# Eight edits to the order of work in a hash-masked attention with a gated feed-forward layer on one core

## The chip, the core and the metric

The kernel runs on one core of a Trainium2 chip. The metric is device time in microseconds (us) of one execution, lower is better. The core has the engines TensorE (PE, with its weight loads shown apart as PEld), VectorE (DVE), ScalarE (ACT), GpSimd (POOL) and SyncE (SP), each with its own queue that is worked off in the order of the program. SP issues most of the transfers (DMAs); POOL issues those of the feed-forward weights.

## The reference

Two stages follow each other. The first is attention in which a query sees only the keys whose six sign bits under a random projection are the same as its own:

```python
q_bits = (einsum('bhsd,dk->bhsk', q, proj) > 0)      # B, H, S, D = 4, 8, 768, 64; six bits
k_bits = (einsum('bhsd,dk->bhsk', k, proj) > 0)
mask = bucket(q_bits)[..., :, None] == bucket(k_bits)[..., None, :]
scores = where(mask, q @ k.T / sqrt(D), -1e9)
attn = softmax(scores);  x = attn @ v                # then heads side by side: 3072 x 512
```

The second is a normalised, gated feed-forward layer on the 3072 rows of x (512 wide, 1536 inside):

```python
xn = x / sqrt(mean(x * x) + 1e-6) * rms_g
out = (silu(xn @ w_gate) * (xn @ w_val)) @ w_out
```

## The kernel before, in words

**Units and slots.** The queries are cut into eight units w of 384 rows (batch w // 2, half w % 2). A unit has eight heads, and a head's 384 queries meet its 768 keys in three slots of two score matmuls (`scores`, L348) and one exponential over 768 columns (`probs`, L358). The 192 slots stand in the list `SLOTS` (L33 to L36); the first units share batches, so their pairs of heads alternate.

**The mask.** It isn't a separate step: twelve rows of sign bits are put below the 64 rows of q and of k in the tile `QK`, so that one matmul over 76 rows gives the score and, for each bit that differs, a large penalty. The bits come from small matmuls into `d_ps` (L214) and a comparison on DVE (`signs`, L221), and they have to be moved to other partitions. For the second, third and fourth pair of heads of batch 1 the function `hash_lone` (L278) moves them with eight transfers on SP (L289), four for each head. The batches before and after have functions of their own.

**Loads.** q and k come as four block transfers a pair of heads each (`load_blocks`, L126), v as one (`load_rows`, L116). DVE turns q and k (`turn_dve`, L198), POOL casts them into `QK` (`cast_pool`, L206). POOL also casts v (`v_prep`, L314) and adds up its rows (`v_sum`, L320 to L322); a matmul with ones makes the mean of v out of these sums (`v_mean`, L329), and DVE scales it into `cvb` (L332). The two halves of w_out are issued by POOL (`load_wo`, L543) in slots 36 and 52.

**Out of the attention.** `av` (L370) multiplies the probabilities with v into the one bank pair `o_ps`. `attn_out` adds `cvb` (L385, DVE), takes a reciprocal (L390, DVE), scales into x (L394) and squares (L406). The last two run on POOL, for the pair "urgent" (unit 0, heads 6 and 7) on DVE, where the squares are added up in the same instruction (L401). `sumsq` (L410, DVE) adds up the squares that POOL made, some slots later.

**The norm and the feed-forward part.** `norm` (L417 on DVE, L419 and L423 on POOL) makes the factors `rstd`; `scale_x` makes `xn` on DVE (L434, or L429 with the gain multiplied in); `turn_x` turns it: four transposes a chunk of 128 rows on PE (L448) with a copy on DVE (L449), or, in the units of `BY_DMA`, for two of three chunks, eight transfers with transposition on SP (L441). Then `gate` (L463 and a tanh on ACT, L465), `value` (L473, with two steps on DVE, L474 and L475) and `project` (L486, a copy on ACT, L493, and a store on SP, L495). All these matmul results share three PSUM banks in rotation (`gps`), so a new one waits until the third one before it has been read.

**The order** is written out by hand. `at(s, f, ...)` puts a step into slot s with a rank; L731 to L741 go through the slots, issue the scores of the next slot, the steps of rank below 3, the exponential, and the other steps in the order of rank and entry. Nothing reorders it afterwards: an instruction that waits holds up all that stands behind it on its engine, and a transfer on SP that waits for its source holds up the transfers behind it. The table `work` (L659) has, for each pair of heads of batches 1 to 3, the slots of its three loads, of its turns and of its hash.

**The tail.** The last 128 rows of the output are made by L743 to L759 in two halves of 256 columns.

Of the kernel before, what the change touches and what calls it, by code (L numbers as in the profile page):

```python
# [40 lines left out]
BY_PE = [(0, hp) for hp in range(4)] + [(1, 0)]  # L41


BY_DMA = (3, 4, 5)


@with_exitstack
def kernel(
# [12 lines left out]
    nc = tc.nc  # L61
# [30 lines left out]
    wo = const.tile([128, NF, DMODEL], FP16, name="wo")  # L92
# [118 lines left out]
    def hash_bank(parts):  # L211
        ps = bank("d_ps", [128, HALF])
        for t, (w, src) in enumerate(parts):
            nc.tensor.matmul(  # L214
                ps[32 * t : 32 * t + 32, :], w, src,
                start=True, stop=True, tile_position=(0, 32 * t),
            )
        return ps

    def signs(bt, ps):  # L220
        nc.vector.tensor_scalar(  # L221
            out=bt, in0=ps, scalar1=thr, scalar2=scl, op0=ALU.is_gt, op1=ALU.mult
        )
# [6 lines left out]
    def bits_tile(i):  # L230

        if i % 2 == 0:
            held.append(spool.tile([128, S], FP16, name="bits", bufs=3))
        return held[-1][:, (i % 2) * HALF : (i % 2 + 1) * HALF]
# [43 lines left out]
    def hash_lone(b, hp):  # L278

        ps = hash_bank(  # L280
            [(w[:, 0:32], T0[b, hp, which][:, half * HALF : (half + 1) * HALF])
             for half in range(2) for w, which in ((pk, "k"), (pq, "q"))]
        )
        bt = bits_tile(0)
        signs(bt, ps)
        for hh in range(2):
            for half, j in ((0, 0), (0, 1), (1, 1), (1, 0)):
                p0, o = 64 * half + 32 * j + 12 * hh, (S, 0)[j] + half * HALF
                nc.sync.dma_start(  # L289
                    out=QK[b, hp][D:KROWS, hh, o : o + HALF], in_=bt[p0 : p0 + 12]  # L290
                )

    def hash_pairs(b, hps):

        bt = spool.tile([128, S], FP16, name="bits", bufs=3)
        for half in range(2):
            cs = slice(half * HALF, (half + 1) * HALF)
            ps = hash_bank(
                [(w, T0[b, hp, which][:, cs])
                 for hp in hps for w, which in ((pk[:, 0:32], "k"), (pq[:, 0:32], "q"))]  # L300
            )
            signs(bt[:, cs], ps)
        for i, hp in enumerate(hps):
            for hh in range(2):
                for j, o in enumerate((S, 0)):
                    p0 = 64 * i + 32 * j + 12 * hh
                    nc.sync.dma_start(
                        out=QK[b, hp][D:KROWS, hh, o : o + S], in_=bt[p0 : p0 + 12]
                    )
# [26 lines left out]
    x, ssp, xn, xnT, ht = {}, {}, {}, {}, {}  # L336
# [41 lines left out]
    def attn_out(w, hp):  # L378
        b = w // 2
        if w not in x:  # L380
            x[w] = xpool.tile([128, 3, DMODEL], FP32, name="x")
            ssp[w] = xpool.tile([128, 3, 4], FP32, name="ssp")
        o = ot.pop((w, hp))
        tmp = spool.tile([128, 3, 2, 66], FP32, name="otmp")
        nc.vector.tensor_add(  # L385
            tmp[:, :, :, 0:65], o[:, :, :, 0:65],
            cvb[b % 2][:, 2 * hp : 2 * hp + 2, 0:65].unsqueeze(1).to_broadcast([128, 3, 2, 65]),
        )
        r = spool.tile([128, 3, 2, 1], FP32, name="rcp")
        nc.vector.reciprocal(r, tmp[:, :, :, 64:65])  # L390
        xd = x[w][:, :, 128 * hp : 128 * hp + 128]
        urgent = (w, hp) == (0, 3)
        eng = nc.vector if urgent else nc.gpsimd
        eng.tensor_mul(  # L394
            xd.rearrange("p c (h d) -> p c h d", h=2), tmp[:, :, :, 0:64],
            r.to_broadcast([128, 3, 2, 64]),
        )
        sq = spool.tile([128, 3, 128], FP32, name="sq")
        if urgent:
            for c in range(3):  # L400
                nc.vector.scalar_tensor_tensor(  # L401
                    out=sq[:, c], in0=xd[:, c], scalar=1.0, in1=xd[:, c],
                    op0=ALU.mult, op1=ALU.mult, accum_out=ssp[w][:, c, hp : hp + 1],
                )
        else:
            nc.gpsimd.tensor_mul(sq, xd, xd)  # L406
        return sq
# [17 lines left out]
    def scale_x(w, c):  # L425
        if w not in xn:
            xn[w] = npool.tile([128, 3, DMODEL], FP16, name="xn")
        if w in BY_DMA and c < 2:
            nc.vector.scalar_tensor_tensor(  # L429
# [6 lines left out]
    def turn_x(w, c):  # L436
        if w not in xnT:
            xnT[w] = npool.tile([128, 4, HALF], FP16, name="xnT", bufs=2)
        if w in BY_DMA and c < 2:
            for kt in range(4):  # L440
# [154 lines left out]
    def at(s, f, *a, rank=3):  # L595
        plan[s].append((rank, len(plan[s]), lambda: f(*a)))
# [4 lines left out]
    moves = {}  # L601
# [54 lines left out]
    def in_row(loads, s, hash_slot=None):  # L656
        return loads, range(s, s + 8), (s + 4, s + 8, s + 9), hash_slot

    work = {  # L659
        (1, 1): in_row((21, 22, 32), 42, 51), (1, 2): in_row((34, 35, 37), 49, 58),  # L660
        (1, 3): in_row((38, 40, 44), 56, 65),
        (2, 0): in_row((53, 55, 59), 64), (2, 1): in_row((66, 67, 68), 73, 82),
        (2, 2): in_row((72, 75, 78), 82), (2, 3): in_row((79, 83, 87), 90, 99),
        (3, 0): in_row((88, 91, 98), 100), (3, 1): in_row((94, 97, 112), 110, 119),
# [2 lines left out]
    for (b, hp), (loads, turns, cast_slots, sh) in work.items():  # L667
        for which, s in zip("kqv", loads):
            at(s, load_rows if which == "v" else load_blocks, nc.sync, b, hp, which)
        for i, s in enumerate(turns):  # L670
            at(s, turn_dve, b, hp, "kq"[i // 4], i % 4, rank=5)
        for which, s in zip("kq", cast_slots):
            at(s, cast_pool, b, hp, which)
        if sh:
            if b == 1:
                at(sh, hash_lone, b, hp)
            else:
                at(sh, hash_pairs, b, (hp - 1, hp))
        at(cast_slots[2], v_prep, b, hp)
        at(cast_slots[2], v_sum, b, hp)  # L680
        if b > 1 and hp % 2:
            at(48 * b + (17 if hp == 3 else -4), v_mean, b, hp - 1, 4)
    for hp, s in enumerate((48, 62, 64, 78)):
        at(s, v_mean, 1, hp, 2)

# [15 lines left out]
    for w in range(8):  # L701
        for h in range(H):
            end = LAST[w, h] + (2 if (w, h) == (0, 7) else 3)
            at(end - 1, av, w, h, 0, 9)
            at(end, av, w, h, 9, 18)
            if h % 2:
                at(end, o_step, w, h // 2, rank=4.5)
                if (w, h) != (0, 7):
                    late = 3 if h == 7 and w < 6 else 5 if (w, h) == (0, 5) else 4
                    at(end + late, s_step, w, h // 2, rank=5 if late != 5 else 4)  # L710
        s0 = 24 * w + 42
        n0 = {0: 11, 2: 7, 3: 13, 4: 13, 5: 13}.get(w, 11)
        at(s0 - n0, norm, w, rank=5)
        for c in range(3):
            scale, rank = {0: 6, 2: 6 - c}.get(w, 8 - c), 1
            turn = {0: (4, 3, 2), 2: (4, 2, 1)}.get(w, (5, 3, 1))[c]
            if w in BY_DMA and c < 2:
                scale, turn, rank = 11 - c, 11 - c, 6
            at(s0 - scale, scale_x, w, c, rank=5)
            at(s0 - turn, turn_x, w, c, rank=rank)  # L720
        seen = set()
        for ft in range(NF):
            for f, s in ((g_step, s0 + 16 * ft // NF), (v_step, s0 + (32 * ft + 16) // (2 * NF))):
                at(s, f, w, ft, rank=4 if s in seen else 2)
                seen.add(s)
        for i in range(9 if w < 7 else 6):
            c, j = divmod(i, 3)
            at(s0 + 16 + i, project, w, c, 4 * j, 4 * j + 4, rank=1 if i == 8 else 3)
# [11 lines left out]
        for _, _, f in todo[n:]:  # L740
            f()  # L741
    rows = out[3 * S : 4 * S, :].rearrange("(p c) n -> p c n", c=6)[:, out_chunk(7, 2), :]
    for i in range(2):  # L743
        cs = slice(256 * i, 256 * i + 256)
        y = bank("y_ps")
        for ft in range(NF):
            nc.tensor.matmul(  # L747
                y[:, cs], ht[7][:, ft, 256:384], wo[:, ft, cs],
                start=(ft == 0), stop=(ft == NF - 1),
            )  # L750
        ysb = spool.tile([128, DMODEL], FP32, name="ysb", bufs=3)
        if i == 0:
            nc.scalar.copy(ysb[:, 0:256], y[:, cs])
            nc.sync.dma_start(out=rows[:, cs], in_=ysb[:, 0:256])
        else:
            nc.scalar.copy(ysb[:, 0:128], y[:, 256:384])
            nc.vector.tensor_copy(ysb[:, 128:256], y[:, 384:512])
            nc.scalar.dma_start(out=rows[:, 256:384], in_=ysb[:, 0:128])
            nc.sync.dma_start(out=rows[:, 384:512], in_=ysb[:, 128:256])  # L759


# [28 lines left out]
```

## Time and profile before

| what | value |
|---|---|
| time, three runs | 334.0, 334.08, 335.57 us; median 334.08 |
| span of the profiled execution, first to last instruction | 332.5 us |
| what lies outside that span, against the median | 1.6 us |
| DVE, ACT, POOL busy | 234.2, 208.0, 157.1 us |
| instructions | 7788 |
| moved by DMA | 32.41 MB, mean 97 GB/s |
| PE work, the largest groups | scores 93.7, v_ps 78.1, y_ps 69.2, g_ps 63.4, o_ps 56.7 us |

"Busy" is the time in which an engine had at least one instruction under way; it says nothing about how fast that instruction ran. A row of the timeline gives start, length, engine, line, operation, the tile written and the tile read, shapes, the count of merged instructions, and in brackets the idle time of the engine ahead of it with what ended it. A row of the chain of waits gives start, length and what the end of the program was waiting for then. "SPq" and "POOLq" are instructions of an engine's sequencer; for a transfer, the length is that of its issue and not that of its landing.

### The profile page before, as it was taken

The numbers are of one execution on the slowest core, as the hardware profiler recorded it, in microseconds if no ns is written. First come the engines' busy times: TensorE is split into PE (matmuls) and PEld (weight loads), VectorE is DVE, ScalarE is ACT, GpSimd is POOL, SyncE is SP. The second block draws the span as 40 slices with busy tenths as digits, with TensorE's granted clock in tenths as the row PEclk, the third lists the DMA queues.
The fourth block names the chain that finished last, engine by engine and source line by source line (L and its number), as shares of the span: only waits on it lengthen the run. The fifth ranks groups of instructions, "written<-read, shape, count | busy, mean of one in ns | idle before, by whom it ended". The sixth has DMA issues, their size and how long they took to land.

```text
span 332.5 us, 7788 instructions
## 1 busy us (share of the span) xinstructions
PE 323.3 (97%) x2959; PEld 198.5 (60%) x2959; DVE 234.2 (70%) x526; ACT 208.0 (63%) x324; POOL 157.1 (47%) x230
## 2 busy tenths in 40 slices
PE   8999989998999999999999999999999999999995
PEld 7576656555566556656565656566566656655653
DVE  3799579997598956989476874977257753793860
ACT  3788977674576665667675766757666766422421
POOL 4887956487747476376744365643110311130000
PEclk9999999999999999999999999999999999999999
DMA  6995997898348927841361714000200001002002
GB/s 221 349 201 151 147 173 140 158 172 134 117 86 156 168 40 174 156 90 24 91 146 34 141 34 150 3 17 18 80 32 2 3 32 65 0 3 82 13 2 95
DMA packets 89956, 32.41 MB, mean 97 GB/s; under 512 B 75336, under 2 KB 86848, under 8 KB 89920
## 3 DMA queue, kind: packets, MB, share of 16 engines
q1 hardware_dynamic: 85984, 27.14, 35.0%
q0 software_dynamic: 3712, 4.72, 9.2%
q8 instruction: 23, 0.38, 0.5%
q14 instruction: 13, 0.11, 0.1%
q10 hardware_dynamic: 224, 0.07, 0.1%
HBM read 28.58 MB, written 6.29 MB: 105 GB/s over the span
## 4 chain that ended last, share of the span: by engine, by line
PE 82%; DVE 5%; DMA 5%; POOL 4%; ACT 1%; issue 1%; SPq 1%; POOLq 0%; DVEq 0%; ACTq 0%
PE v_ps L473 17%; PE y_ps L486 16%; PE s_ps L348 15%; PE g_ps L463 14%; PE o_ps L370 9%; PE s_ps L463 4%; PE d_ps L214 3%; DMA QK<-bits 3%; PE t_ps L174 2%; DMA kL<-in_k_dram 1%; PE z_ps L341 1%; PE x_ps L448 1%; DVE t L474 1%; PE y_ps L747 1%; POOL sq L406 1%
## 5 line engine op out<-in xcount | busy, mean ns | idle before, releaser
L358 ACT ACTIVATE psb<-s_ps 128x768 f16<-128x768 f32 x192 | 150.6, 809 | 31.9 <-PE s_ps L348 29.9
L348 PE MATMUL s_ps<-QK 76*128 76x384 f16 x384 | 93.7, 325 | 2.5 <-DMA QK<-bits 1.3
L473 PE MATMUL v_ps<-xnT,wv 128*128 128x384 f16 x384 | 78.1, 325 | 0.0
L486 PE MATMUL y_ps<-wo,ht 128*128 128x512 f16 x276 | 69.2, 378 | 0.0
L394 POOL TENSOR_TENSOR x<-otmp,rcp 128x384 f32<-128x384 f32 x31 | 26.1, 843 | 84.8 <-DVE rcp L390 84.6
L370 PEld LDWEIGHTS <-psb 128*128 128x128 f16 x1152 | 52.2, 97 | 22.0 <-issue 3.6
L465 ACT ACTIVATE t<-g_ps 128x384 f32<-128x384 f32 x78 | 38.3, 491 | 43.2 <-PE g_ps L463 42.7
L463 PE MATMUL g_ps<-xnT,wg 128*128 128x384 f16 x312 | 63.4, 325 | 0.3
L474 DVE SCALAR_TENSOR_TENSOR t<-t,g_ps 128x384 f32<-128x384 f32 x78 | 42.7, 547 | 28.8 <-ACT t L465 28.4
L475 DVE SCALAR_TENSOR_TENSOR ht<-t,v_ps 128x384 f16<-128x384 f32 x96 | 53.2, 554 | 10.4 <-PE v_ps L473 0.9
L370 PE MATMUL o_ps<-vl,psb 128*128 128x65 f16 x1152 | 56.7, 193 | 0.3 <-DVE otmp L385 0.3
L463 PEld LDWEIGHTS <-wg 128*128 128x128 f16 x384 | 36.0, 97 | 24.1 <-issue 0.7
L473 PEld LDWEIGHTS <-wv 128*128 128x128 f16 x384 | 36.2, 97 | 23.2
L348 PEld LDWEIGHTS <-QK 76*128 76x128 f16 x384 | 31.3, 98 | 19.3 <-issue 4.7
L486 PEld LDWEIGHTS <-ht 128*128 128x128 f16 x276 | 26.0, 97 | 26.3 <-issue 1.9
L493 ACT COPY ysb<-y_ps 128x512 f32<-128x512 f32 x23 | 13.5, 587 | 24.6 <-PE y_ps L486 24.1
L406 POOL TENSOR_TENSOR sq<-x 128x384 f32<-128x384 f32 x31 | 26.3, 849 | 2.4
L385 DVE TENSOR_TENSOR otmp<-o_ps,cvb 128x390 f32<-128x390 f32 x32 | 17.9, 559 | 12.6 <-PE o_ps L370 12.5
L206 POOL CAST QK<-qT 64x768 f16<-64x768 f32 x22 | 18.1, 823 | 15.8 <-DVE qT L198 15.1
L206 POOL CAST QK<-kT 64x768 f16<-64x768 f32 x22 | 18.5, 841 | 13.6 <-PE m_ps L329 3.8
L449 DVE TENSOR_TENSOR xnT<-x_ps,gcol 128x512 f16<-128x512 f16 x18 | 12.2, 683 | 14.1 <-PE x_ps L448 14.0
L198 DVE STREAM_TRANSPOSE kT<-kL 128x192 f32<-128x192 f32 x44 | 21.7, 515 | 0.0
(81 smaller groups left out, 297.6 us busy)
## 6 DMA issues: line engine op xcount, KB each, us to landing
vL<-in_v_dram SPq DMA_DIRECT2D x16, 384.0 KB
out_dram<-ysb SPq DMA_DIRECT2D x23, 256.0 KB
kL<-in_k_dram SPq DMA_DIRECT2D x44, 96.0 KB
qL<-in_q_dram SPq DMA_DIRECT2D x44, 96.0 KB
kL<-in_k_dram SPq DMA_DIRECT2D x4, 384.0 KB
qL<-in_q_dram SPq DMA_DIRECT2D x4, 384.0 KB
wg<-in_moe_w_gate_dram POOLq DMA_DIRECT2D x2, 768.0 KB, 8.2
wv<-in_moe_w_val_dram POOLq DMA_DIRECT2D x2, 768.0 KB, 9.3
```

The lines of the kernel that those rows point to most:

```text
L206: nc.gpsimd.tensor_copy(QK[b, hp][0:64, hh, o : o + S], T0[b, hp, which][64 * hh : 64 * hh + 64, :])
L348: nc.tensor.matmul(ps[:, j, 0:HALF], k_cols(w // 2, h, 2 * p + j), q_cols(w, h), start=True, stop=True,)
L358: nc.scalar.activation(psb[w, h][:, p], sps.pop(g)[:, :, 0:HALF], AF.Exp, scale=ESCALE,)
L370: nc.tensor.matmul(o[:, c, hh, 0:65], psb[w, h][:, jt // 2, jt % 2, 128 * c : 128 * c + 128], vls[b % 2][:, h, v_chunk(b, h, jt), 0:65], s ...
L394: eng.tensor_mul(xd.rearrange("p c (h d) -> p c h d", h=2), tmp[:, :, :, 0:64], r.to_broadcast([128, 3, 2, 64]),)
L406: nc.gpsimd.tensor_mul(sq, xd, xd)
L463: nc.tensor.matmul(g, wg[:, kt, fs], xnT[w][:, kt], start=(kt == 0), stop=(kt == 3))
L465: nc.scalar.activation(t, g, AF.Tanh, scale=0.5)
L473: nc.tensor.matmul(vv, wv[:, kt, fs], xnT[w][:, kt], start=(kt == 0), stop=(kt == 3))
L474: nc.vector.scalar_tensor_tensor(out=t, in0=t, scalar=1.0, in1=g, op0=ALU.add, op1=ALU.mult)
L475: nc.vector.scalar_tensor_tensor(out=ht[w][:, ft], in0=t, scalar=0.5, in1=vv, op0=ALU.mult, op1=ALU.mult)
L486: nc.tensor.matmul(y, ht[w][:, ft, c * 128 : (c + 1) * 128], wo[:, ft, :], start=(ft == 0), stop=(ft == NF - 1),)
```

## The change

Nothing is computed differently except where a step runs. The edits are these:

- **A.** Heads 4 and 5 of unit 0 become "urgent" too: their scaling and squares go from POOL to DVE, and their `sumsq` step (L410), which stood in DVE's queue just ahead of L385 of heads 6 and 7, goes away.
- **B.** `hash_lone` sends only the first head's four transfers itself; the second head's four are entered with rank 3.5 in the same slot. The loads of q and v of the pair (1, 3) move from slots 40 and 44 to 51 and 52. On SP this gives, ahead of the second turn of batch 1: the load of k (four transfers), the bits of the first head (four), the load of q (four), the bits of the second head (four), the load of v. Before it was k, q, v and then the eight transfers of bits. For the other two pairs the order on SP stays the same.
- **C.** `v_prep` and `v_sum` of the pair (2, 1) move two slots later, behind L419 and L423 of unit 2 on POOL.
- **D.** The first `v_mean` of batches 2 and 3 moves four slots earlier (from 92 to 88 and from 140 to 136), out of the stretch in which gates and values rotate through the three banks.
- **E.** Unit 6 joins `BY_DMA`: two of its three chunks are turned by eight transfers on SP; eight transposes on PE and two copies on DVE go away. Its `norm` is entered two slots earlier, its last `sumsq` one slot earlier.
- **F.** The tail is cut into 256, 128 and 128 columns, each with a bank, a result tile and a store of its own: 36 matmuls and weight loads in place of 24. The first two stores are issued by ACT, the last by SP.

```diff
-BY_DMA = (3, 4, 5)
+BY_DMA = (3, 4, 5, 6)
...
-        for hh in range(2):
+
+        def send(hh):
             for half, j in ((0, 0), (0, 1), (1, 1), (1, 0)):
                 p0, o = 64 * half + 32 * j + 12 * hh, (S, 0)[j] + half * HALF
                 nc.sync.dma_start(
                     out=QK[b, hp][D:KROWS, hh, o : o + HALF], in_=bt[p0 : p0 + 12]
                 )
+
+        send(0)
+        return send
...
-        urgent = (w, hp) == (0, 3)
+        urgent = (w, hp) in ((0, 2), (0, 3))
...
-        (1, 3): in_row((38, 40, 44), 56, 65),
+        (1, 3): in_row((38, 51, 52), 56, 65),
...
-                at(sh, hash_lone, b, hp)
+                at(sh, lambda b=b, hp=hp: moves.update({(b, hp): hash_lone(b, hp)}))
+                at(sh, lambda b=b, hp=hp: moves[b, hp](1), rank=3.5)
...
-        at(cast_slots[2], v_prep, b, hp)
-        at(cast_slots[2], v_sum, b, hp)
+        late = 2 if (b, hp) == (2, 1) else 0
+        at(cast_slots[2] + late, v_prep, b, hp)
+        at(cast_slots[2] + late, v_sum, b, hp)
         if b > 1 and hp % 2:
-            at(48 * b + (17 if hp == 3 else -4), v_mean, b, hp - 1, 4)
+            at(48 * b + (17 if hp == 3 else -8), v_mean, b, hp - 1, 4)
...
-                if (w, h) != (0, 7):
-                    late = 3 if h == 7 and w < 6 else 5 if (w, h) == (0, 5) else 4
-                    at(end + late, s_step, w, h // 2, rank=5 if late != 5 else 4)
+                if (w, h) not in ((0, 5), (0, 7)):
+                    late = 3 if h == 7 and w < 7 else 4
+                    at(end + late, s_step, w, h // 2, rank=5)
...
-        n0 = {0: 11, 2: 7, 3: 13, 4: 13, 5: 13}.get(w, 11)
+        n0 = {0: 11, 2: 7, 3: 13, 4: 13, 5: 13, 6: 13}.get(w, 11)
...
-    for i in range(2):
-        cs = slice(256 * i, 256 * i + 256)
+    for lo, hi in ((0, 256), (256, 384), (384, 512)):
         y = bank("y_ps")
...
+        copy, queue = (nc.vector.tensor_copy, nc.sync) if hi == 512 else (nc.scalar.copy, nc.scalar)
+        copy(ysb[:, lo:hi], y[:, lo:hi])
+        queue.dma_start(out=rows[:, lo:hi], in_=ysb[:, lo:hi])
```

More of the change, by code (lines that the diff above doesn't have):

```diff
@@ L747 @@
             nc.tensor.matmul(
-                y[:, cs], ht[7][:, ft, 256:384], wo[:, ft, cs],
+                y[:, lo:hi], ht[7][:, ft, 256:384], wo[:, ft, lo:hi],
                 start=(ft == 0), stop=(ft == NF - 1),
@@ L751 @@
         ysb = spool.tile([128, DMODEL], FP32, name="ysb", bufs=3)
[L752 to L759, printed above, removed]
+        copy, queue = (nc.vector.tensor_copy, nc.sync) if hi == 512 else (nc.scalar.copy, nc.scalar)
+        copy(ysb[:, lo:hi], y[:, lo:hi])
+        queue.dma_start(out=rows[:, lo:hi], in_=ysb[:, lo:hi])
 _INS = ['q', 'k', 'v', 'proj', 'moe_w_gate', 'moe_w_val', 'moe_w_out', 'moe_rms_g']
```

## The prediction, as it was put on record

> **What bounds the kernel now.** I read the page first, then the chain of waits, then the timeline wherever the chain leaves TensorE.
>
> ```profile
> span 332.5 us, 7788 instructions
> ...
> PE 323.3 (97%) x2959; PEld 198.5 (60%) x2959; DVE 234.2 (70%) x526; ACT 208.0 (63%) x324; POOL 157.1 (47%) x230
> ...
> PE 82%; DVE 5%; DMA 5%; POOL 4%; ACT 1%; issue 1%; SPq 1%; POOLq 0%; DVEq 0%; ACTq 0%
> ```
>
> ```profile
> core 0: 332.5 us, clock 0.998
> ```
>
> TensorE is busy 97% of the span and carries 82% of the chain; 332.5 - 323.3 = 9.2 us are all that its waits can be worth by this view. So an edit pays only where it ends a wait of TensorE or takes work from it. The sum below is made on the profiled execution, span 332.5; the median of the runs, 334.08, has 1.6 us outside that span, which no edit touches, so savings are taken off 334.08. The measurement can tell a difference of about 0.5% (1.67 us) from none.
>
> **The change part by part.** *A, squares of heads 4 and 5 on VectorE.* The timeline around the first norm:
>
> ```profile
> 38.80 0.29 DVE L332 TENSOR_SCALAR cvb<-m_ps 128x130 f32<-128x130 f32 x1 [1.61 <-PE m_ps L329]
> ...
> 39.20 0.44 PE L370 MATMUL o_ps<-vl,psb 128*128 128x65 f16 x9
> ...
> 39.78 0.82 POOL L406 TENSOR_TENSOR sq<-x 128x384 f32<-128x384 f32 x1
> ...
> 40.63 0.55 DVE L410 TENSOR_REDUCE ssp<-sq 128x3 f32<-128x384 f32 x1 [1.54 <-POOL sq L406]
> ...
> 41.10 0.55 DVE L385 TENSOR_TENSOR otmp<-o_ps,cvb 128x390 f32<-128x390 f32 x1
> ...
> 41.91 0.56 DVE L394 TENSOR_TENSOR x<-otmp,rcp 128x384 f32<-128x384 f32 x1
> ...
> 43.26 0.17 DVE L417 TENSOR_REDUCE ss<-ssp 128x3 f32<-128x12 f32 x1
> ...
> 43.89 0.89 POOL L423 TENSOR_TENSOR rstd<-ms,mhalf 128x3 f32<-128x3 f32 x1
> ...
> 44.75 0.99 POOL L543 DMA_DIRECT2D wo<-in_moe_w_out_dram  x1
> 44.81 1.53 DVE L434 TENSOR_SCALAR xn<-x,rstd 128x512 f16<-128x512 f32 x3 [0.76 <-POOL rstd L423]
> 45.36 0.40 PE L448 MATMUL x_ps<-ident,xn 128*128 128x128 f16 x4 [0.61 <-DVE xn L434]
> ...
> 46.39 1.51 ACT L358 ACTIVATE psb<-s_ps 128x768 f16<-128x768 f32 x2 [0.74 <-PE s_ps L348]
> ...
> 47.47 0.43 PE L370 MATMUL o_ps<-vl,psb 128*128 128x65 f16 x9 [0.34 <-DVE otmp L385]
> ...
> 48.87 0.81 PE L463 MATMUL g_ps<-xnT,wg 128*128 128x384 f16 x4
> ```
>
> VectorE's queue is in order: L385 of heads 6 and 7 could have started when their matmuls ended (39.20 + 0.44 = 39.64), but stood behind L410, which waited 1.54 for POOL's squares, and started at 41.10. With L410 gone it starts 41.10 - 39.64 = 1.4 earlier, and so do the sums, POOL's rstd and xn. VectorE's new work, 0.56 for L394 and, from its end at 42.47 to 43.26, 0.79 for the squares, fits the idle 1.61 ahead of L332; if that cover were gone, L332 and L385 would come later by what sticks out, at most 1.35. On TensorE the idle 0.61 (x_ps) and 0.34 (o_ps, behind VectorE's late xn work) end, with the gates behind them: 0.95, and some 0.15 of restart, so I take **-1.1**. Above stands 1.4, the whole shift; below stands 0, if the exponentials were the limit, which the idle 0.74 of ACT beside it speaks against. POOL's queue moves with it: the issue of w_out at 44.75 comes 1.3 earlier too (see the rival on the slower side).
>
> *B, one head's bits ahead of q.* SP's queue and the two score matmuls that depend on it:
>
> ```profile
> 62.27 3.08 SPq L126 DMA_DIRECT2D kL<-in_k_dram  x4
> 65.85 2.66 SPq L126 DMA_DIRECT2D qL<-in_q_dram  x4
> ...
> 69.29 6.20 SPq L289 DMA_DIRECT2D QK<-bits  x8
> 75.54 2.71 SPq L126 DMA_DIRECT2D kL<-in_k_dram  x4
> ...
> 81.11 6.18 SPq L289 DMA_DIRECT2D QK<-bits  x8
> ```
>
> ```profile
> 68.75 0.89 POOL L543 DMA_DIRECT2D wo<-in_moe_w_out_dram  x1
> ...
> 76.65 0.48 PE L348 MATMUL s_ps<-QK 76*128 76x384 f16 x2 [0.94 <-DMA QK<-bits]
> ...
> 85.63 0.49 PE L348 MATMUL s_ps<-QK 76*128 76x384 f16 x2
> ```
>
> ```profile
> 70.99 5.53 DMA QK<-bits
> ```
>
> TensorE stands still 0.94 at 76.65 for bits whose transfers SP began only at 69.29, behind q and v, and which took 5.53 to land beside the second half of w_out (issued 68.75). After the change they go right behind k, which ends at 62.27 + 3.08 = 65.35: the first head's four take 6.20 / 8 x 4 = 3.1, to 68.45. Even with the 5.53 the third of them lands before 74, ahead of TensorE at 76.65 - 1.1 - 0.9. So **-1.0** (0.94 and its restart). q now starts about 68.5 instead of 65.85, the second head's bits end about 74.2 instead of 75.49, v goes last.
>
> What is late next: from 69.29 on SP issues without a pause, and the order behind 75.54 is unchanged, so SP doesn't get earlier with TensorE. The matmul at 85.63 needs the first three transfers of the group begun at 81.11: issued by 81.11 + 3 x 0.77 = 83.4. They landed between that and 85.63, since no wait shows there; I take the middle, 84.5. TensorE, 2.1 earlier, would be there at 83.5. So **+1.0** comes back (0 if SP itself runs ahead; 2.1, all of A and B, if they landed only just in time).
>
> *C, casts and sums of v behind the third norm.*
>
> ```profile
> 116.45 0.82 POOL L314 CAST vl<-vL 128x768 f16<-128x768 f32 x1
> ...
> 117.24 0.99 POOL L320 TENSOR_TENSOR vadd<-vL 128x384 f32<-128x384 f32 x1
> ...
> 119.66 0.86 POOL L423 TENSOR_TENSOR rstd<-ms,mhalf 128x3 f32<-128x3 f32 x1
> ...
> 121.10 0.40 PE L448 MATMUL x_ps<-ident,xn 128*128 128x128 f16 x4 [0.59 <-DVE xn L434]
> ```
>
> The four POOL steps from 116.45 stood ahead of the norm; rstd comes more than 2 us earlier and the idle 0.59 ends: **-0.6** (0 to -0.75 with restart). The sums are then ready near 121 and wanted by the moved mean two slots after 121.10, some 2 us cover; without it the mean would wait.
>
> *D, means out of the gates.* The chain at the first of the two places:
>
> ```profile
> 132.06 0.40 DVE t L474
> 132.46 0.04 issue
> 132.50 0.81 PE g_ps L463 x4
> ```
>
> A gate waits for a bank that VectorE reads late, because the mean took one of the three. The timeline shows no idle row there, so the wait is short: 0.15 at each of two places, **-0.3** (0 to twice the 0.40 of L474). The mean's own work moves, hidden nowhere, and costs the same.
>
> *E, unit 6 turned by transfers.* Stretches of the same fourteen slots in unit 5 (turned by transfers) and in unit 6, between score matmuls, from the windows view (length, then busy time and count of each engine):
>
> ```profile
> 222.09:243.15 21.06, 21.06 (x188) 12.56 (x186) 9.91 (x21) 14.12 (x22) 5.44 (x7) 1.00 0.15 42
> 258.19:279.67 21.48, 21.48 (x195) 12.94 (x193) 10.44 (x22) 14.21 (x23) 5.04 (x7) 1.00 0.07 26
> ```
>
> ```profile
> 227.00 10.05 SPq L441 DMA_TRANSPOSE xnT<-xn  x8
> ```
>
> TensorE is full in both; the difference is **-0.4** (0, to -0.8 if the eight transposes cost twice that). Unit 5's eight issues end at 237.05, 6 us before its stretch does; unit 6's have the same place, and only stores behind them on SP.
>
> *F, tail.*
>
> ```profile
> 329.38 0.29 DVE L757 COPY ysb<-y_ps 128x128 f32<-128x128 f32 x1 [7.06 <-ACT ysb L756]
> ```
>
> VectorE's last copy waits for ACT's copy of the same bank and starts 0.3 later. With banks of their own it follows the last matmul: **-0.3** (+0.5 if twelve more weight loads show, -0.6 if the stores split better).
>
> Sum: -1.1 - 1.0 + 1.0 - 0.6 - 0.3 - 0.4 - 0.3 = -2.7, so 334.08 - 2.7 = **331.4**; its own range is 330.8 to 332.3.
>
> **The rivals.** *Nothing is held up at 85.63* (SP ahead of its old pace, since A also moves w_out's first half): the +1.0 goes, 330.4.
>
> The Trainium skill speaks for this one: "DMA: Bandwidth & Descriptors", section "Queues, rings and completion order", says that each DMA engine goes round the queues that have work, a packet at a time; by that q would share with w_out and land, and the time would be about 330.4. The 5.53 for a few KB of bits beside w_out agrees badly with it.
>
> *SP governs the whole stretch*: all of A and B comes back, 334.08 - 1.6 = 332.5. For it: SP's rows from 69.29 touch each other. Against it: no bits but those at 76.65 made TensorE wait there.
>
> *q runs into w_out* (slower than before). Four block loads issued just behind a weight load:
>
> ```profile
> 32.43 6.44 SPq L126 DMA_DIRECT2D kL<-in_k_dram  x4
> ...
> 38.98 7.11 SPq L126 DMA_DIRECT2D qL<-in_q_dram  x4
> ```
>
> They took 6.44 and 7.11 on SP instead of 2.66. Before, q was issued by 68.5, ahead of w_out at 68.75; after, q starts near 68.5 and w_out, moved by A, near 67.6. If q's issue stalls as at 38.98, everything on SP behind it is about 4.1 later: the bits for 85.63 land at 84.5 + 4.1 = 88.6, TensorE is 3.0 later than before instead of 1.1 earlier, and with C to F: 334.08 + 3.0 - 1.6 = 335.5. It decides as soon as q's stall passes the slack: it is slower than before from a stall of 2.7 on. Against it: here one load meets the weights, with nothing of its kind still queued; at 38.98 there were k's blocks too.
>
> TensorE would then stand idle for about 5 us. The Trainium skill, "TensorE: Matmul & The Clock Gate", Part 1, has the clock halved after an idle window of about 3.4 us; by that the estimate would be some 1.7 us more, 337.2. No run here shows such a stop, and the granted clock before is 0.998 throughout, so I leave it out of the sum.
>
> **How the numbers follow.** Forecast 331.4: 0.46. Nothing held up, 330.4: 0.18. SP governs, 332.5: 0.15. q runs into w_out, 335.5: 0.16. Left over, 0.05, for unit 6's transfers or the means coming late. The range leaves out q's case and the rest: from 329.9 (the first rival with A at its bound) to 333.3 (the third case with D and F at nothing), close to 0.8. Faster by over 0.5% means below 332.41: the forecast and the first rival, and a third of "SP governs": 0.69. Within 0.5%, up to 335.75: the rest of that and most of q's case: 0.20. Slower: 0.11.
>
> **What would show each step.** A: L385 near 39.7, no idle ahead of x_ps, gates starting near 47.8. B: no wait for bits at the second turn; q's four issues in under 3 us; a wait of up to 1 us at the third turn. C: rstd ahead of vadd and no idle at x_ps. D: no VectorE in the chain near 130 and 205. E: stretches of units 5 and 6 alike. F: VectorE's last copy without a wait for ACT. I am wrong if q's issue takes 6 us or more, or if TensorE waits for bits or turned q for more than 2 us anywhere between 60 and 100.

## The result, and the profile after

| | median | runs | against before, 95% interval |
|---|---|---|---|
| before | 334.08 us | 332.56 to 336.34 | |
| after | 337.81 us | 336.43 to 338.33 | 1.0093 [1.0064, 1.0121] |
| after, once more | 338.14 us | 336.12 to 339.73 | 1.0105 [1.0068, 1.0142] |

The change is slower by about 1%, 3.7 us; the forecast was 331.4. Where a kernel's runs spread by more than 1.5%, its ratio is taken from the faster of them; medians are over all its runs.

L289 of before is L290 here, and later lines are four higher (one more in act and act_wo). The page, the cores view and the waits of TensorE, of the kernel after:

```profile
span 336.5 us, 7812 instructions
...
PE 324.6 (96%) x2963; PEld 199.1 (59%) x2963; DVE 235.5 (70%) x530; ACT 207.8 (62%) x324; POOL 156.3 (46%) x228
...
PEclk9999999999789999999999999999999999999999
```

```profile
core 0: 336.5 us, clock 0.990
```

```profile
PE s_ps L352 <- DMA QK<-bits: 4.3, 1, 4.3
PE y_ps L490 <- DMA wo<-in_moe_w_out_dram: 1.1, 1, 1.1
```

Two waits that before did not have, and a clock row with two slices under full speed right behind them (the eleventh and twelfth, 84 to 101 us). The next two views are SP's queue and TensorE at those places:

```profile
62.04 3.04 SPq L126 DMA_DIRECT2D kL<-in_k_dram  x4
65.58 3.20 SPq L290 DMA_DIRECT2D QK<-bits  x4
68.88 6.74 SPq L126 DMA_DIRECT2D qL<-in_q_dram  x4
75.67 3.14 SPq L290 DMA_DIRECT2D QK<-bits  x4
78.92 0.46 SPq L116 DMA_DIRECT2D vL<-in_v_dram  x1
79.42 2.90 SPq L126 DMA_DIRECT2D kL<-in_k_dram  x4
82.36 2.71 SPq L126 DMA_DIRECT2D qL<-in_q_dram  x4
85.19 6.89 SPq L290 DMA_DIRECT2D QK<-bits  x8
```

```profile
74.19 0.49 PE L352 MATMUL s_ps<-QK 76*128 76x384 f16 x2
...
76.21 0.59 PE L490 MATMUL y_ps<-wo,ht 128*128 128x512 f16 x2 [1.10 <-DMA wo<-in_moe_w_out_dram]
...
88.91 0.80 PE L352 MATMUL s_ps<-QK 76*128 76x384 f16 x2 [4.32 <-DMA QK<-bits]
```

The second turn (74.19) no longer waits for bits, as B intends. But q, issued at 68.88, a microsecond after POOL issued w_out's second half (67.77), holds SP for 6.74 instead of 2.66: its four issues follow each other without a pause and take 0.65, 1.07, 2.16 and 2.73. Everything behind it is 4.1 late, the bits for the third turn are issued at 85.19 instead of 81.11, and TensorE stands still for 4.32. After that the scores take 0.80 instead of 0.49: half clock. Nothing of this is at the end of the program, and the third turn is where all of the loss arises. The start of the score matmuls of some slots, from the timeline, against before (us; the runs below the first row are the experiments):

| kernel | 38 | 44 | 60 | 61 | 65 | 66 | 68 | 87 | 191 |
|---|---|---|---|---|---|---|---|---|---|
| after | -0.14 | -1.39 | -2.46 | -1.21 | -1.20 | +3.28 | +5.84 | +5.84 | +4.20 |
| no_a (B to F) | -0.67 | -0.65 | -1.71 | -1.70 | -1.64 | +3.32 | +5.85 | +5.85 | +4.21 |
| no_b (A, C to F) | -0.74 | -1.99 | +0.83 | +0.83 | +0.83 | +1.25 | +1.24 | +1.35 | -0.29 |
| no_ab (C to F) | -0.09 | -0.07 | -0.97 | -0.81 | -0.81 | -0.81 | -0.82 | -0.82 | -2.45 |
| no_wo | -0.73 | -1.98 | -3.10 | -3.10 | -3.10 | -1.70 | -1.71 | -1.71 | -3.34 |
| no_wo_b | -0.62 | -1.87 | -1.94 | -1.94 | -1.94 | -0.11 | -0.12 | -0.12 | -1.75 |
| no_wo_ab | -0.62 | -0.62 | -1.66 | -1.66 | -1.66 | -1.66 | -1.66 | -1.66 | -3.29 |
| reorder | -0.74 | -1.99 | -2.87 | -1.63 | -1.63 | -1.63 | -1.63 | +4.40 | +2.76 |

The column of slot 38 is what the first loads of that execution differed by, ahead of every edit.

### The profile page after: what moved, and what is told of

It reads as the page before. It is cut to its first block, busy times and chain, and to the rows that moved or that the text cites. A ratio compares the mean times of both kernels' runs of the same rounds, so it can differ in the third digit from the quotient of the medians.

```text
span 336.5 us, 7812 instructions
## 1 busy us (share of the span) xinstructions
PE 324.6 (96%) x2963; PEld 199.1 (59%) x2963; DVE 235.5 (70%) x530; ACT 207.8 (62%) x324; POOL 156.3 (46%) x228
## 4 chain that ended last, share of the span: by engine, by line
PE 85%; POOL 5%; SPq 3%; DMA 2%; DVE 2%; ACT 2%; issue 1%; DVEq 0%; POOLq 0%; ACTq 0%
PE v_ps L477 17%; PE s_ps L352 17%; PE y_ps L490 16%; PE g_ps L467 14%; PE o_ps L374 9%; PE d_ps L214 4%; PE s_ps L467 3%; SPq L126 2%; PE t_ps L174 2%; POOL QK L206 1%; ACT psb L362 1%; PE z_ps L345 1%; PE x_ps L452 1%; DMA kL<-in_k_dram 1%; POOL x L398 1%
## 5 line engine op out<-in xcount | busy, mean ns | idle before, releaser
L490 PE MATMUL y_ps<-wo,ht 128*128 128x512 f16 x276 | 70.3, 382 | 1.1 <-DMA wo<-in_moe_w_out_dram 1.1
L389 DVE TENSOR_TENSOR otmp<-o_ps,cvb 128x390 f32<-128x390 f32 x32 | 17.9, 559 | 15.5 <-PE o_ps L374 15.5
L410 POOL TENSOR_TENSOR sq<-x 128x384 f32<-128x384 f32 x30 | 25.5, 849 | 2.4
L198 DVE STREAM_TRANSPOSE qT<-qL 128x192 f32<-128x192 f32 x44 | 21.3, 517 | 1.9 <-DMA qL<-in_q_dram 1.9
```

The costliest lines, as they stand in the source:

```text
L198: nc.vector.transpose(dst.rearrange("p (c t r) -> p r c t", c=6, r=4)[:, r : r + 1], src.rearrange("p (r c) d -> p r c d", r=4)[:, r : r + 1],
L490: nc.tensor.matmul(y, ht[w][:, ft, c * 128 : (c + 1) * 128], wo[:, ft, :], start=(ft == 0), stop=(ft == NF - 1),)
```

## The experiments

**Which part does it: A and B apart.** B undone (no_b, first diff), A undone (no_a, second diff; the `sumsq` step of heads 4 and 5 is entered again), both undone (no_ab).

```diff
-        (1, 3): in_row((38, 51, 52), 56, 65),
+        (1, 3): in_row((38, 40, 44), 56, 65),
...
         send(0)
-        return send
+        send(1)
```

```diff
-        urgent = (w, hp) in ((0, 2), (0, 3))
+        urgent = (w, hp) == (0, 3)
```

no_b: 

> The kernel after with B undone (q and v of the pair (1,3) loaded in slots 40 and 44 again, all eight bit transfers behind them), A and C to F kept. Theory (B puts q's four block loads right behind the second half of w_out, where they get nothing until it has landed): q's issue takes 2.7 us again instead of 6.74, the wait of 4.3 for bits at the third turn is gone, the clock stays near 0.998. The wait for bits at the second turn comes back, and as SP doesn't get earlier with A it is 0.94 + 1.2 = about 2.1 us there. Time: before less C to F (1.85) and at most a part of A: 331.5 to 332.5 us. Rival (A is the cause, since it alone moves w_out's second half 1 us earlier onto the loads): the third turn waits 2 us or more and the time stays above 336.

no_a: 

> The kernel after with A undone (heads 4 and 5 scaled and squared on POOL again), B and C to F kept. Theory (B alone suffices): q still starts within a microsecond of w_out's second half, its issue takes 6 us or more, the third turn waits about 4 us for bits, the clock halves; what A gained was given back before the third turn anyway, so the time is that of after, 337.3 to 338.5 us. Rival (it takes A and B together: without A w_out comes 1.0 later and q is ahead of it again): q's issue takes under 4 us, no wait at the third turn, 332 to 333 us.

no_ab: 

> The kernel before with C to F alone. Theory (C to F are worth what the slots of the two traces showed, 0.76 + 0.14 + 0.30 + 0.45 + 0.2 = 1.85): 332.2 us, and up to slot 80 the same as before. Rival (some of C to F only filled room that the late third turn had made): nearer to 334.

| | with A | without A |
|---|---|---|
| with B | 337.81 (after) | 338.63, 1.0115 [1.0084, 1.0147] |
| without B | 333.81, 0.9983 [0.9964, 1.0003] | 332.51, 0.9941 [0.9912, 0.9969] |

B alone makes the stall: without A q takes 6.65 and the third turn waits 4.79, so the rival that it takes both falls. C to F alone give 1.97 us, as expected in time; but up to slot 80 they were to run as before, and from slot 60 on this execution is 0.8 to 1.0 ahead, for it has no wait at the second turn. In the trace C to F themselves give 1.8. But A alone isn't free: its median is 1.3 us above that of C to F, with intervals that hardly overlap, and 333.8 instead of the 331.5 to 332.5 expected. SP and TensorE without B:

```profile
67.91 0.89 POOL L547 DMA_DIRECT2D wo<-in_moe_w_out_dram  x1
```

```profile
68.54 0.58 SPq L116 DMA_DIRECT2D vL<-in_v_dram  x1
69.23 8.34 SPq L290 DMA_DIRECT2D QK<-bits  x8
```

```profile
77.48 0.48 PE L352 MATMUL s_ps<-QK 76*128 76x384 f16 x2 [3.11 <-DMA QK<-bits]
```

q is quick again (2.66 at 65.78), but v and the bits now follow w_out's issue. The wait at the second turn isn't the 2.1 expected but 3.11, more than all of A's gain. What ended it is in the chain of waits and in the waits of SP:

```profile
70.92 6.42 DMA QK<-bits
```

```profile
SPq L290 <- DMA vL<-in_v_dram: 2.2, 1, 2.2
```

The third bit transfer is issued at 70.92, as early as before (70.99), but takes 6.42 to land instead of 5.53. The 8.34 isn't what TensorE waited for. Seven of the eight transfers are issued at the pace of before, 0.71 to 0.83 each; then SP stands for 2.2 ahead of the eighth, which belongs to the second head (its issue starts at 76.86). In this trace a transfer of SP waits on the semaphore of the one issued eight before it, here v's, which landed at 76.84, 8.3 after its issue.

The granted clock adds to A's price here: eight of the ten runs of no_b have a mean of 0.995, as one period of 3.41 us at half clock in 332 us would give, though the profiled one has none.

**Is it w_out?** The kernel after without the second half's transfer, then with B, and with A and B, taken out. The products use the first half of w_out twice, so the output is another one.

```diff
-        at(36 + 16 * i, load_wo, 6 * i, 6 * i + 6)
+        if i == 0:
+            at(36, load_wo, 0, 6)
-                y, ht[w][:, ft, c * 128 : (c + 1) * 128], wo[:, ft, :],
+                y, ht[w][:, ft, c * 128 : (c + 1) * 128], wo[:, ft % 6, :],
```

no_wo: 

> The kernel after without the transfer of w_out's second half; all products with w_out use its first six chunks twice, so the output is another one and one transfer of 1.57 MB is left out, the instructions of all engines otherwise the same. Theory (q starves because w_out's second half takes the DMA engines): q's four issues take 2.7, the wait of 1.1 for w_out and that of 4.3 for bits are gone, slot 66 is 2.5 ahead of before, the clock stays up; 334.4 - 2.4 - 1.85 = about 330. Rival (q stalls behind its own buffers or SP's own full queue): q's issue stays over 5 us and the third turn waits 2 us or more.

no_wo_b: 

> No transfer of w_out's second half (its products use the first six chunks twice, another output), A and C to F kept, B undone. Theory (without w_out beside them the eight bits go in 6.2 and B is worth what the wait at the second turn was, up to 1.0): a wait of 1 to 2 us for bits at the second turn; but as the run without w_out and with B still lost 1.4 at the third turn to SP, the times are equal within 0.5: 332.0 to 332.8. Rival (B is worth its 1.0): 333.5.

no_wo_ab: 

> As the last, with A undone too. Theory (SP's pace, which neither A nor B changes, sets the third turn): again within 0.7 us of the run without w_out's second half that has A and B, 332 to 333. Rival (A and B are worth 2 us when w_out is out of the way): 334.5.

Measured: 332.62 (0.9960 [0.9928, 0.9991]), 331.67 (0.9929 [0.9897, 0.9961]), 331.96 (0.9926 [0.9890, 0.9961]). SP and TensorE of no_wo:

```profile
67.91 2.71 SPq L126 DMA_DIRECT2D qL<-in_q_dram  x4
70.66 3.14 SPq L290 DMA_DIRECT2D QK<-bits  x4
...
80.22 6.21 SPq L290 DMA_DIRECT2D QK<-bits  x8
```

```profile
83.93 0.48 PE L352 MATMUL s_ps<-QK 76*128 76x384 f16 x2 [1.23 <-DMA QK<-bits]
```

The same q at the same place takes 2.71 when w_out isn't there: w_out's transfer (768 KB by the profile, not the 1.57 MB of the expectation) is what starves it. The wait for w_out and the half clock go too. But the time is 332.6, not 330: TensorE still waits 1.23 at the third turn, and starts there at -1.70, which is where the kernel without A and B (-1.66) starts without any wait. The medians say much the same: they lie within 1 us of each other with overlapping intervals, so without w_out's second half neither A nor B shows a gain, and A's price of 1.3 is gone too (331.67 with it, 331.96 without). That SP's own pace sets the third turn fits, but this pace differs with the execution: no_wo_b starts slot 66 at -0.11. The wait of 1 to 2 us that no_wo_b was to show at the second turn didn't come; it waited 1.67 at the third, and its median lies just under the range expected.

The Trainium skill, "DMA: Bandwidth & Descriptors", section "Queues, rings and completion order", lets the engines go round the queues a packet at a time, by which q would share. 6.74 against 2.71 shows how little of a share that was here. The queues of the kernel after from 69.6 to 74 us (packets, MB, the packets' own times as a share of the 16 DMA engines; w_out is on q0, SP's loads on q1):

```profile
q0 software_dynamic: 657, 0.67, 109.5%
q1 hardware_dynamic: 95, 0.02, 3.8%
```

Whether a packet of the profile is one of that page, no run shows.

**Move w_out.** One slot later without B (hold, first diff), and in slot 50 behind the cast of q with B (wo_early, second diff).

```diff
-        at(36 + 16 * i, load_wo, 6 * i, 6 * i + 6)
+        at((36, 53)[i], load_wo, 6 * i, 6 * i + 6)
```

```diff
-        at(36 + 16 * i, load_wo, 6 * i, 6 * i + 6)
+        at((36, 50)[i], load_wo, 6 * i, 6 * i + 6, rank=(3, 3.5)[i])
```

hold: 

> The run without B (A and C to F, order k, q, v, bits as before), with the second half of w_out one slot later, so that A doesn't move it ahead of its old time: about 69.5 instead of 67.91. Theory (A lost 2 us in the run without B because w_out came 0.8 earlier and the eight bit transfers, 8.34 us instead of 6.2, fell into it): the bits issue in under 7 us, the wait for bits at the second turn falls from 3.11 to about 2, w_out's wait adds at most 1; 332.3 to 333.3 us. Rival (what A wins is lost at the second turn whatever w_out does): as without B, 333.8, or more because w_out itself is late.

wo_early: 

> The kernel after with only the second half of w_out issued in slot 50 behind the cast of q, near 62.2 instead of 67.77. Theory (q starves only while w_out is under way): q starts near 70 with 1 or 2 us of w_out left, its issue takes 3 to 4 us instead of 6.74, the wait at the third turn falls from 4.3 to about 2 (SP stays behind because k stalls instead), the clock stays up or nearly; 332 to 334 us. Rival (the time of w_out's issue doesn't matter, SP is simply full): third turn and time as in the kernel after, 337 or more.

hold gave 335.27 (0.9998 [0.9960, 1.0037]) and doesn't decide: POOL came to the issue at 68.06, hardly later than 67.91, the bits took 9.47 (with pauses of SP for q and v in it, and 7.10 to land for the third), and the wait was 4.46. wo_early's median is 337.64, the rival's number, but its four runs (332.58, and three of 337.6 to 338.0) are too few and too far apart to settle it. In the profiled one, of 337.69, q is quick now, but the load and the bits ahead of it aren't:

```profile
62.07 5.70 SPq L126 DMA_DIRECT2D kL<-in_k_dram  x4
68.28 4.58 SPq L290 DMA_DIRECT2D QK<-bits  x4
72.97 2.71 SPq L126 DMA_DIRECT2D qL<-in_q_dram  x4
...
85.11 6.21 SPq L290 DMA_DIRECT2D QK<-bits  x8
```

The stall moves from q to k and the bits, and the third turn's bits start at 85.11 as after (85.19). In these orders SP loses 2 to 4 us to w_out's transfer: 4.1 after, 2.1 in no_b (8.34 - 6.20), 3.3 in hold, 4.0 here (5.70 + 4.58 in place of 3.04 + 3.20). It isn't so in every order: in before and in no_ab, where v is issued ahead of w_out, the eight bits beside it take 6.20 and 6.23.

**Take the third turn's bits out of the jam.** On ACT's queue (act, first diff), the same with w_out early (act_wo), or ahead of the loads of pair (2,0) on SP (reorder, second diff), the same with w_out early (reorder_wo).

```diff
-                nc.sync.dma_start(
+                eng = nc.scalar if (hp, hh) == (2, 0) else nc.sync
+                eng.dma_start(
```

```diff
-        (2, 0): in_row((53, 55, 59), 64), (2, 1): in_row((66, 67, 68), 73, 82),
+        (2, 0): in_row((58, 59, 60), 67), (2, 1): in_row((66, 67, 68), 73, 82),
```

act: 

> The kernel after, but the first head's four bit transfers for the third turn, pair (1,2), are issued by ACT in slot 58 instead of by SP. q's load still stalls behind w_out, w_out still lands when it did. Theory (the third turn waits only because these transfers stand in SP's queue behind the stalled q and two more block loads: the comparison that makes the bits ends about 74, SP sends them at 85.19): the wait of 4.3 goes, the clock stays up, the loss of 7.05 at the third turn goes with them, about 331 us; only the wait of 1.1 for w_out at the second turn and small waits for q behind stay. Rival (the late q itself would hold the third turn or the one after it, through the turns on VectorE, and ACT's queue pays for the issues): 334 us or more, with another wait in the place of this one.

act_wo: 

> As the run with ACT, and the second half of w_out is issued in slot 50 behind the cast of q instead of slot 52, about 62.2 instead of 67.77, so that it lands near 71. Theory (w_out's landing, not the bits, set the second turn in the kernel after): the wait of 1.1 for w_out goes too, slot 61 is 2.4 ahead of before; 329.5 to 330.5 us if the loads that it now meets (k and q ahead of the second turn) have that much slack. Rival (whatever SP issues during these 8 us stalls, and k of (1,3) with the first head's bits is now hit instead): a wait for bits of the second turn of 1 us or more, 332 us or more.

reorder: 

> The kernel after with the loads of pair (2,0) entered in slots 58, 59, 60 instead of 53, 55, 59, and its turns and casts three slots later, so that on SP the first head's four bit transfers for the third turn go ahead of k and q of (2,0) instead of behind them. No transfer is added or leaves SP. Theory (the third turn waits only for those four, which were ready near 74 and issued at 85.19): they are issued near 79.4 and land by 84, TensorE comes at 84.4, the wait is 0 to 0.5, the clock stays up; the 1.2 of slot 65 is kept, 334.4 - 1.2 - 1.85 = about 331.4, and q's stall of 6 us or more is still there and costs nothing more. Rival (with SP full, something behind it is late instead: the turns of (2,0) or the bits of (1,3)): a new wait of 2 us or more after slot 66, 333 or more.

reorder_wo: 

> As the run with (2,0) behind, and w_out's second half issued in slot 50 behind the cast of q, near 62. Theory: the wait for w_out in slot 61 is gone as well, slot 65 is 1.6 ahead of before as in the run with w_out early, no wait at the third turn: 330.8 to 331.3. Rival (the bits of the second turn or the turns of k are late by the stall that moves onto k): 331.4 or more, no better than without.

Measured: act 334.41 (1.0013 [0.9979, 1.0047]), act_wo 334.78 (1.0009 [0.9987, 1.0031]), reorder 336.94 (1.0076 [1.0047, 1.0106]), reorder_wo 336.33 (0.9982 [0.9942, 1.0023]; its runs, 332.1 to 339.3, lie too far apart to place it). In all four profiles the wait at the third turn is gone, as the theory says; no median comes to the 329.5 to 331.4 expected. ACT of the run act:

```profile
74.02 3.66 ACTq L291 DMA_DIRECT2D QK<-bits  x4
77.79 1.51 ACT L363 ACTIVATE psb<-s_ps 128x768 f16<-128x768 f32 x2 [4.92 <-POOL vadd L326]
```

Four issues hold ACT's exponentials for 3.66, w_out's wait is 1.86 there, and a half-clock period follows: slot 63 is at +0.93. In act_wo the issues hold ACT for 3.69, and slots 61 to 63 lose 3.8. In reorder SP serves the third turn in time and the fourth late:

```profile
68.49 6.66 SPq L126 DMA_DIRECT2D qL<-in_q_dram  x4
...
79.02 3.06 SPq L290 DMA_DIRECT2D QK<-bits  x4
```

```profile
97.53 0.48 PE L352 MATMUL s_ps<-QK 76*128 76x384 f16 x2 [2.22 <-DMA QK<-bits]
...
106.88 1.35 PE L477 MATMUL v_ps<-xnT,wv 128*128 128x384 f16 x4 [1.82 <-DVE t L478]
```

That is the rival put beside it: with SP full, what is taken from one transfer is paid by the next. Slots 72 to 80 lose 3.65 there, with a period of half clock behind the second of these waits.

**The half clock.** Seventy filler matmuls, no part of the computation, in the third turn's wait.

```diff
-        idle(ps[:, 0, HALF:512], {0: 8, 3: 6}.get(g, 0))
+        idle(ps[:, 0, HALF:512], {0: 8, 3: 6, 66: 70}.get(g, 0))
```

warm: 

> The kernel after with 70 matmuls of 128 columns, whose results nobody reads, put ahead of the scores of slot 66, where TensorE stands idle 4.3 us. They aren't part of the computation. Theory (the idle time lets the clock fall to half, which costs 2.5 us beyond the wait itself): no half clock in the record, the scores behind the wait take 0.49 us instead of 0.80, the time is 2.0 to 2.5 us under after, 335.3 to 335.8. Rival (the halved matmuls are hidden, the next stage waits for the late bits and loads anyway): the clock stays up and the time is within 0.5 us of after.

after_2: 

> The kernel after once more, to stand beside the filler matmuls in the same call: about 337.8 us, clock 0.99.

warm_2: 

> The 70 filler matmuls ahead of the scores of slot 66 once more. Theory (half clock costs 2.5 us): 2.0 to 2.5 us under the kernel after of this call, and in the trace the loss from slot 65 to slot 68 is about 4.4 instead of 7. Rival (half the clock costs little): within 1 us of it.

Medians: 337.10 and 337.27, beside 337.81 and 338.14 for the kernel after: 0.7 and 0.9 less, not the 2.0 to 2.5 expected. It is what warm_2's rival said, and the intervals overlap (1.0081 [1.0052, 1.0110] and 1.0105 [1.0068, 1.0142] against before). The traces show a part of why. In the first the fillers reached up to the bits, no half clock followed there, and slots 65 to 68 lost 4.3 (after: 7.0, of which 5.84 - 3.28 = 2.56 behind the wait; 2.13 in after_2). But that execution is the slowest of its ten, 339.01: q took 8.17, w_out was waited for 2.15 at the second turn, and the half clock came there. In the second they ended too early, and the half clock came all the same; slots 65 to 68 lost 7.5:

```profile
82.69 4.07 PE L345 MATMUL s_ps<-ones 128*128 128x128 f16 x70
88.52 0.48 PE L352 MATMUL s_ps<-QK 76*128 76x384 f16 x2 [1.76 <-DMA QK<-bits]
```

So in the two profiles of the kernel after the two periods of half clock cost 2.1 to 2.6 us behind the wait, and the fillers kept them away from the third turn in one of the two profiles. What the half clock is worth in the time of the whole is open: 12 of the 18 filler runs show a mean clock of 0.998 or more, and their median, 337.0, is only 1.0 under that of the 16 runs of the kernel after, none of which is over 0.994.

**The better version.** no_ab_2: 

> C to F alone once more, to stand beside the two versions above under the same runs of before: 332.5 as in its first runs, a ratio of 0.994.

332.41, 0.9943 [0.9905, 0.9980]; with its first runs (0.9941) C to F alone are 0.6% faster than before and some 1.5% faster than after.

## Why the prediction was wrong

The case that came was the third rival, "q runs into w_out", with the halved clock beside it (337.2), at a chance of 0.16. By the steps of the text:

- **A, -1.1: right in size.** Slot 44 stands 1.39 earlier, 0.14 of it from the loads: 1.25. The rows, L389 and the first gate:

```profile
39.53 0.56 DVE L389 TENSOR_TENSOR otmp<-o_ps,cvb 128x390 f32<-128x390 f32 x1 [0.35 <-PE o_ps L374]
```

```profile
47.47 0.81 PE L467 MATMUL g_ps<-xnT,wg 128*128 128x384 f16 x4
```

They were forecast near 39.7 and 47.8.
- **B, -1.0: the wait went, and in this execution 1.25 came back one slot later.** The step named the bits of the third turn as what is late next, and not w_out's second half, which slot 61 needs. That wait differs with the execution: 1.25 here, 0.16 in after_2, 2.39 in warm, whose queue up to there is the same. And the 0.94 was no fixed property of the kernel: the two profiles of C to F, with B's order undone, show no wait at the second turn. One execution had been read as the rule.
- **The failed step is q's price.** The text took 2.66 for q behind the bits and let the second head's bits end about 74.2; it took 6.74, and they ended at 78.81. So SP was 4.08 late with the bits of the third turn, and TensorE waited 4.32 for them. The argument "here one load meets the weights, with nothing of its kind still queued" set aside the stall that the rows at 32.43 and 38.98 showed. One load of four transfers beside w_out is enough (6.74 after, 6.65 in no_a, 2.71 without w_out). Bit transfers are issued beside it at nearly their old pace, but land late.
- **+1.0 given back at 85.63: the right place, the wrong size.** It became 7.05: 4.5 of wait and restart, and 2.6 of half clock. The rival's sum had 4.1 for SP's delay, measured 85.19 - 81.11 = 4.08. Its 335.5 lacked mainly the clock; the estimate of 1.7 for that was too low, since the clock stayed down for two periods.
- **Nothing held up (0.18) and SP governs (0.15)** didn't come. SP governs came near the truth where w_out is out of the way: without its second half, slot 66 starts at -1.66 with neither A nor B and at -1.70 with both, though at -0.11 with A alone. By the text's own terms the ends of its range are 330.1 and 333.1, not 329.9 and 333.3; that changes nothing.
- **C to F: right.** Slot 88 shows -0.76 for C (forecast -0.6), slots 94 and 150 -0.14 and -0.30 for D (-0.15 each), E -0.45 (-0.4), the tail -0.15 (-0.3): 1.8 against 1.6. For E, the two stretches of units 5 and 6 that differed by 0.42 are now alike:

```profile
226.74:247.80 21.06, 21.06 (x188) 12.56 (x186) 9.91 (x21) 14.11 (x22) 5.44 (x7) 1.00 0.15 42
262.84:283.90 21.06, 21.06 (x188) 12.49 (x186) 9.60 (x20) 14.22 (x23) 5.45 (x7) 1.00 0.13 38
```

The sum of the trace: -0.14 - 1.25 - 1.10 + 1.25 + 7.05 - 0.76 - 0.44 - 0.45 - 0.15 = +4.0, the spans' 336.5 - 332.5.

How far A itself slows SP is open. In the profiles with A, SP starts q of pair (1,2) between 57.3 and 59.4, in those without it between 54.9 and 58.0. w_out's first half, which POOL issues near 44.4 without A and near 42.8 with it, would explain it; no run moved that half alone.

## What to carry to other kernels

When a queue issues without a pause over tens of microseconds, an edit that brings its consumer forward gained little here, and most of the new orders tried only chose who waits. Look at a queue's transfers one by one: a row that merges eight of them hides what it waited for in between. Before a load is moved, look at what the other queues move at its new time, and price it by the worst row in which the two have met, not by its row when alone. And ask of every wait that an edit removes what else ends at that same moment, and whether a second execution shows the wait at all.

## What the runs showed of the hardware

The granted clock changes on a grid of 3.41 us, and a stop much shorter than that is enough. The windows view, in stretches of 3.41 us laid by the clock's own changes (columns: length, PE busy, weight loads, DVE, ACT, POOL, granted clock, DMA share, GB/s), of the kernel after, of no_b (laid by the change at its span's end), of warm_2 and of act:

```profile
84.20:87.61 3.41, 0.39 (x10) 0.26 (x8) 0.52 (x1) 0.03 (x1) 3.29 (x4) 1.00 0.72 107
87.61:91.02 3.41, 2.11 (x14) 0.85 (x14) 0.69 (x1) 0.81 (x1) 0.95 (x3) 0.50 0.07 16
91.02:94.43 3.41, 3.41 (x20) 1.48 (x17) 1.10 (x2) 0.00 (x0) 0.00 (x0) 0.50 0.32 83
94.43:97.85 3.42, 3.42 (x29) 2.03 (x28) 1.13 (x3) 1.91 (x4) 0.00 (x0) 1.00 0.57 202
```

```profile
72.69:76.10 3.41, 1.69 (x21) 0.72 (x13) 3.31 (x8) 0.51 (x1) 3.29 (x5) 1.00 1.13 238
76.10:79.52 3.42, 2.04 (x19) 1.20 (x20) 1.87 (x4) 0.86 (x2) 3.20 (x5) 1.00 0.15 26
```

```profile
86.54:89.95 3.41, 1.65 (x19) 0.65 (x16) 0.68 (x1) 0.81 (x1) 0.45 (x1) 1.00 0.05 11
89.95:93.37 3.42, 3.42 (x21) 1.67 (x18) 1.11 (x3) 0.00 (x0) 0.00 (x0) 0.50 0.31 73
```

```profile
74.48:77.89 3.41, 1.55 (x16) 0.80 (x15) 1.50 (x3) 0.10 (x1) 3.19 (x6) 1.00 0.52 80
77.89:81.30 3.41, 3.41 (x13) 1.64 (x12) 2.22 (x5) 2.81 (x4) 1.59 (x3) 0.50 0.13 25
```

A period with PE busy for 1.65 or 1.55 of its 3.41 us was followed by one at half clock; one with 1.69 was not, although the stop in no_b (3.11) was longer than that in warm_2 (1.76): it lay across the edge between two periods. Between 1.65 and 1.69, about half a period, lies the bound in these runs: of some 1700 periods at full clock in the eighteen profiles, all 18 with PE busy for 1.66 or less (seven of them at the program's end) were followed by half clock, and none of the others. In the kernel after, a period of 2.11 busy at half clock didn't bring the clock back; the next one, busy throughout, did. Where the grid lies differs from one execution to the next, which may be why no_b's ten runs have mean clocks of 0.995 (eight) and 1.0 (two); that wasn't tried. The Trainium skill, "TensorE: Matmul & The Clock Gate", Part 1, has a free-running window of about 3.4 us, which the trace agrees with; that it takes an idle window, the trace doesn't: half a window was enough.
